# Attention and an MLP-mixer in one kernel: the first pass in another order

## The chip, the cores and the metric

The kernel runs on one core of a Trainium2 chip. The metric is the device time of one execution in microseconds, lower is better. Engines are named as in the profile: PE is TensorE's matmul, PEld its weight load, DVE is VectorE, ACT is ScalarE, POOL is GpSimd and SP is SyncE, which here only issues DMAs.

## The reference

```python
# q, k, v: (8, 8, 576, 64) float32, g_norm: (64,); the mixer's four weights are float64
kv  = einsum('bhsd,bhse->bhde', k, v)
out = einsum('bhsd,bhde->bhse', q, kv)
rms = sqrt(mean(out * out, axis=-1) + 1e-6)
x   = (out / rms * g_norm) as (8, 576, 512)        # heads side by side
h   = maximum(x.T @ w_tok1, 0) @ w_tok2            # over the 576 tokens; 256 wide
u   = x + h.T
y   = u + maximum(u @ w_ch1, 0) @ w_ch2            # over the 512 channels; 1536 wide
```

## The kernel before, in words

**First stage.** Batches are taken two at a time: four pairs. Of each batch, 512 rows lie in four tiles of 128, and the remaining 64 rows of both batches of a pair share a fifth. `attention(pair)` has nine steps. `kv(side, half)` multiplies half of the heads' k and v (`ps_kv`), copies the two diagonal blocks into `kvp` (one copy on DVE, one on ACT), and asks for the next k and v (`load(n + 2)`; two buffers each). `attend(c)` is 8 matmuls into `ps_o` for two row tiles; `attend_rem` does the shared tile. Each ends in `norm`: a square on ACT, a sum, a root with one step of correction and a product on DVE, the product with `g_norm` on POOL. That gives one tile of `X`.

`token_mixing(pair)` has 11 steps: `tok1(t)`, for half of the 256 columns, sums over all row tiles of both batches and over the shared tile into `ps_h`, then applies the maximum on ACT (`h1`); `tok2(i)` makes row tile i of u in `ps_u`, DVE adds X, and a DMA stores u in `u_dram`.

**The weights** arrive as float64. `decode` rounds a block to float32: a scaled copy on ACT, a clip on POOL (L134), four operations on DVE (L136, L138, L140, L142) and a last add on POOL (L144). The raw blocks come by DMAs on ACT's queue into two buffers (`raw`). Both channel products use a 2 x 2 scheme with seven products, for which `mix_ch1` and `mix_ch2` form four sums each of the rounded weights, on POOL (L185, 1536 columns each).

**Order of the first stage.** `weave(body, fill)` writes body's steps and spreads the others between them. The first attention is woven with the token weights, then the mixing of pair p with the attention of pair p + 1, and over the three of these the blocks of w_ch1 (eight of 768 columns), `mix_ch1`, the blocks of w_ch2 (twelve of 512), `mix_ch2`. The last mixing is woven with the first transposes of u. A scheduler may then move instructions on an engine; the order of each engine is fixed when the program is built, and each engine works through its own in that order.

**Channel stage.** Nine groups of 512 rows of u: `channel1` for three parts of the hidden width (`ps_v`), then `channel2` (`ps_w`), with the transposes of the next group between.

Of the kernel before, what the change touches and what calls it, by code (L numbers as in the profile page):

```python
# [9 lines left out]
F32 = mybir.dt.float32  # L10
# [7 lines left out]
def kernel(  # L18
# [55 lines left out]
    dram = ctx.enter_context(tc.tile_pool(name="dram", bufs=1, space=bass.MemoryType.DRAM))  # L74
    right = ExitStack()
# [26 lines left out]
    def w_psum(shape, name):  # L102
        return ps_w.tile(shape, F32, name=name, tag="w")

# [3 lines left out]
    def load(n):  # L108
# [40 lines left out]
    def fetch(n):  # L149
        return stage.tile([P, n, 2], U32, name="raw", tag="raw")  # L150

    def get_tok1(j, n):
        raw = fetch(n * DTOK)
        w = words(moe_w_tok1)
        if j < J:
            nc.scalar.dma_start(raw.rearrange("p (j n) w -> p j n w", j=n),
                                w[ds(j * P, n * P)].rearrange("(j p) n w -> p j n w", p=P))
        else:
            nc.scalar.dma_start(raw[:HF], w[LO:])
            nc.scalar.dma_start(raw[HF:], w[LO:])  # L160
        decode(w_tok1[:, j:j + n].rearrange("p j n -> p (j n)"), raw)

    def get_tok2(t):
        raw = fetch(S)
        nc.scalar.dma_start(raw, words(moe_w_tok2)[ts(t, P)])
        decode(w_tok2[:, t], raw)
# [6 lines left out]
    def get_ch1(i, c):  # L173
        raw = fetch(FH)
        nc.scalar.dma_start(raw, words(moe_w_ch1)[ts(c, P), ts(i, FH)])
        decode(w_ch1[:, A1[i, c // 2], c % 2], raw)

    def get_ch2(f):
        raw = fetch(DM)
        nc.scalar.dma_start(raw, words(moe_w_ch2)[ts(f, P)])  # L180
        a, b = B2[f // NS, 0], B2[f // NS, 1]
        decode(w_ch2[:, a:b + 1:b - a, f % NS], raw.rearrange("p (h n) w -> p h n w", h=2))

    def combine(o, a, b, op):
        nc.gpsimd.tensor_tensor(out=o, in0=a, in1=b, op=op)  # L185

    def mix_ch1():
        w = [w_ch1[:, i] for i in range(7)]
# [5 lines left out]
    def mix_ch2():  # L194

        w = [w_ch2[:, i] for i in range(7)]
# [12 lines left out]
    def attention(pair):  # L209
        def kv(side, half):  # L210
            n = 4 * pair + 2 * side + half
            kk, vv = k_in[n % 2], v_in[n % 2]
            ps = w_psum([P, 2, P], "ps_kv")
            for i in range(2):
                for j in range(JJ):
                    nc.tensor.matmul(ps[:, i], lhsT=kk[:, j, ts(i, P)], rhs=vv[:, j, ts(i, P)],  # L216
                                     start=(j == 0), stop=(j == JJ - 1))
            dst = kvp[side][:, 2 * half:2 * half + 2]
            nc.vector.tensor_copy(dst[:HF, :, :D], ps[:HF, :, :D])
            nc.scalar.copy(dst[HF:, :, D:], ps[HF:, :, D:])  # L220
# [25 lines left out]
        def attend(c):  # L246
            side = c // 2
            ps = ps_o.tile([P, 2, DM], F32, name="ps_o", tag="o")
            for t in range(2):
                for hp in range(HP):  # L250
                    nc.tensor.matmul(ps[:, t, ts(hp, P)],  # L251
                                     lhsT=qT[2 * pair + side][:, hp, ts(2 * (c % 2) + t, P)],
                                     rhs=kvp[side][:, hp], start=True, stop=True)
            norm(ps, c, 2)

        def attend_rem():
            ps = ps_o.tile([P, 1, DM], F32, name="ps_o", tag="o")
            for hp in range(HP):
                for side in range(2):
                    nc.tensor.matmul(ps[ds(side * HF, HF), 0, ts(hp, P)],  # L260
                                     lhsT=qT[2 * pair + side][:, hp, LO:],
                                     rhs=kvp[side][:, hp], start=True, stop=True)
            norm(ps, 4, 1)

        return [do(kv, 0, 0), do(kv, 0, 1), do(attend, 0), do(kv, 1, 0), do(attend, 1),
                do(kv, 1, 1), do(attend_rem), do(attend, 2), do(attend, 3)]


    def token_mixing(pair):
        h1 = {}  # L270

        def tok1(t):
            ps = []
            for side in range(2):
                if t == 0:
                    h1[side] = hp_.tile([P, NTOK, DM], F32, name="h1")
                ps.append(w_psum([P, DM], "ps_h"))
                for j in range(J):
                    nc.tensor.matmul(ps[side], lhsT=w_tok1[:, j, ts(t, P)],  # L279
                                     rhs=x_of(pair, side * J + j), start=(j == 0), stop=False)  # L280
            for side in range(2):
                r = ds(side * HF, HF)
                nc.tensor.matmul(ps[side], lhsT=w_tok1[r, J, ts(t, P)], rhs=x_of(pair, 8)[r],
                                 start=False, stop=True)
            for side in range(2):
                nc.scalar.activation(h1[side][:, t], ps[side], AF.Relu)  # L286

        def tok2(i):
            ps = w_psum([P, DM], "ps_u")
            if i < 8:  # L290
                for t in range(NTOK):
                    nc.tensor.matmul(ps, lhsT=w_tok2[:, t, ts(i % J, P)], rhs=h1[i // J][:, t],  # L292
                                     start=(t == 0), stop=(t == NTOK - 1))
            else:
                for t in range(NTOK):
                    for side in range(2):
                        nc.tensor.matmul(ps[ds(side * HF, HF)], lhsT=w_tok2[:, t, LO:],
# [3 lines left out]
            nc.vector.tensor_tensor(out=x, in0=ps, in1=x, op=ALU.add)  # L301
# [7 lines left out]
        return [do(tok1, t) for t in range(NTOK)] + [do(tok2, i) for i in range(9)]  # L309
# [9 lines left out]
    def turn_u(g, i, psum):  # L319
        if i == 0:  # L320
            uT[g] = late["u"].tile([P, NC, J * P], F32, name="uT")
        ps = psum()
        for c in range(NC):
            nc.tensor.transpose(ps[:, c], xg[g][:, i, ts(c, P)], ident)  # L324
        nc.scalar.copy(uT[g][:, :, ts(i, P)], ps)  # L325
# [216 lines left out]
```

## Time and profile before

| | us |
|---|---|
| runs | 976.95, 981.16, 983.23 (median 981.16) |
| profiled execution | 976.97 |
| its span | 975.2 |
| PE busy | 896.6 (92%) |
| DVE busy | 383.1 (39%) |
| POOL busy | 246.2 (25%) |
| ACT busy | 148.5 (15%) |
| first matmul of the channel stage | 302.2 |

The span is the time from the first to the last instruction. Shares are of the whole span, of which the channel stage is the larger part; a share within the first stage has to be read from a window of it. A busy PE may run at a lower granted clock, which is listed apart. HBM traffic of the whole span is 52.85 MB read and 18.87 MB written.

### The profile page before, as it was taken

The page shows a single profiled execution, that of the slowest core. Times are in us where ns is not written, and L with a number is a line of the kernel's source. Part 1 is how long each engine was busy: PE and PEld are TensorE (multiplying, and loading weights), DVE is VectorE, ACT ScalarE, POOL GpSimd, SP SyncE. Part 2 cuts the span into 40 slices and gives each one's busy share as a digit, 9 for nine tenths or more (in the row PEclk, how much of TensorE's full clock was granted, in tenths as well). Part 3 has the DMA queues.
Part 4 walks back from the last instruction along what each step waited for, and adds up shares of the span by engine and source line. Part 5 has one row for each costly group of instructions (what it writes and reads, how often), then busy time and mean ns, then how long its engine had stood idle before and what let it go on. Part 6 is the DMA issues. An engine that isn't in the chain of part 4 may idle for free.

```text
span 975.2 us, 10020 instructions
## 1 busy us (share of the span) xinstructions
PE 896.6 (92%) x4128; PEld 723.8 (74%) x4128; DVE 383.1 (39%) x573; ACT 148.5 (15%) x252; POOL 246.2 (25%) x169
## 2 busy tenths in 40 slices
PE   3749669769999999999999999999999999999997
PEld 2525434535636888888888888888888888888886
DVE  2876887791724303413413412312313312312421
ACT  1321211211211101201201201200210210210210
POOL 2464666470210220220220220220220220220220
PEclk9879879889999999999999999999999999999999
DMA  9955654553332002002002002002002001001001
GB/s 263 317 170 175 223 196 152 189 199 95 118 133 76 1 1 87 1 1 87 1 0 87 1 1 87 1 1 85 3 1 76 10 1 44 1 1 44 1 1 43
DMA packets 42413, 72.37 MB, mean 74 GB/s; under 512 B 2560, under 2 KB 20992, under 8 KB 42368
## 3 DMA queue, kind: packets, MB, share of 16 engines
q1 hardware_dynamic: 38352, 56.63, 17.6%
q10 hardware_dynamic: 4016, 15.11, 4.7%
q8 instruction: 32, 0.52, 0.2%
q14 instruction: 13, 0.11, 0.0%
HBM read 52.85 MB, written 18.87 MB: 74 GB/s over the span
## 4 chain that ended last, share of the span: by engine, by line
PE 78%; DVE 11%; DMA 4%; POOL 4%; issue 1%; ACT 1%; SPq 0%; ACTq 0%; DVEq 0%; POOLq 0%
PE ps_v L365 33%; PE ps_w L404 33%; PE ps_u L292 3%; DMA raw<-in_moe_w_ch_dram 3%; PE ps_h L279 3%; PE ps_kv L216 2%; DVE part L142 2%; PE ps_ut L324 2%; POOL w_ch L185 1%; POOL x L244 1%; DVE x L243 1%; PE ps_o L251 1%; DVE w_ch L138 1%; DVE part L140 1%; DVE ms L230 1%
## 5 line engine op out<-in xcount | busy, mean ns | idle before, releaser
L365 PE MATMUL ps_v<-uT,w_ch 128*128 128x256 f32 x864 | 201.3, 379 | 0.0
L404 PE MATMUL ps_w<-w_ch,vs 128*128 128x256 f32 x864 | 192.1, 379 | 0.0
L365 PEld LDWEIGHTS ps_v<-uT,w_ch 128*128 128x128 f32 x864 | 164.1, 190 | 23.1 <-issue 0.8
L404 PEld LDWEIGHTS ps_w<-w_ch,vs 128*128 128x128 f32 x864 | 162.3, 190 | 21.1
L393 POOL TENSOR_TENSOR vs<-vs,v 128x512 f32<-128x512 f32 x27 | 47.6, 1764 | 428.3 <-DVE vs L389 410.4
L365 PE MATMUL ps_v<-t,w_ch 128*128 128x256 f32 x648 | 153.1, 379 | 0.0
L404 PE MATMUL ps_w<-w_ch,v 128*128 128x256 f32 x648 | 144.1, 379 | 0.0
L365 PEld LDWEIGHTS ps_v<-t,w_ch 128*128 128x128 f32 x648 | 123.1, 190 | 16.7
L404 PEld LDWEIGHTS ps_w<-w_ch,v 128*128 128x128 f32 x648 | 122.5, 190 | 16.3
L279 PE MATMUL ps_h<-x,w_tok 128*128 128x512 f32 x128 | 65.5, 654 | 16.4 <-POOL x L244 16.4
L369 DVE TENSOR_TENSOR v<-ps_v,u 128x512 f32<-128x512 f32 x54 | 37.3, 692 | 102.1 <-PE ps_v L365 102.1
L251 PE MATMUL ps_o<-kvp,qT 128*128 128x128 f32 x256 | 40.2, 319 | 30.4 <-DVE x L243 17.7
L409 POOL TENSOR_TENSOR xg<-xg,u 128x512 f32<-128x512 f32 x27 | 33.8, 1266 | 135.3 <-DVE u L408 135.3
L251 PEld LDWEIGHTS ps_o<-kvp,qT 128*128 128x128 f32 x256 | 37.7, 228 | 40.5 <-issue 23.0
L279 PEld LDWEIGHTS ps_h<-x,w_tok 128*128 128x128 f32 x128 | 25.0, 208 | 52.9 <-issue 29.0
L292 PE MATMUL ps_u<-h,w_tok 128*128 128x512 f32 x128 | 61.8, 614 | 1.4 <-ACT h L286 1.4
L408 DVE TENSOR_TENSOR xg<-ps_w,xg 128x512 f32<-128x512 f32 x27 | 18.7, 692 | 104.9 <-PE ps_w L404 104.9
L244 POOL TENSOR_TENSOR x<-x,g_sb 128x1024 f32<-128x1024 f32 (+1 forms) x20 | 44.2, 2210 | 61.4 <-DVE x L243 58.6
L216 PEld LDWEIGHTS ps_kv<-v_in,k_in 128*128 128x128 f32 x320 | 41.0, 206 | 20.8 <-issue 19.5
L216 PE MATMUL ps_kv<-v_in,k_in 128*128 128x128 f32 x320 | 42.1, 291 | 13.9 <-DMA v_in<-in_v_dram 13.9
L325 ACT COPY uT<-ps_ut 128x512 f32<-128x512 f32 x36 | 21.1, 586 | 213.2 <-PE ps_ut L324 213.2
L408 DVE TENSOR_TENSOR u<-ps_w,u 128x512 f32<-128x512 f32 x18 | 12.4, 692 | 87.2 <-PE ps_w L404 87.2
(62 smaller groups left out, 680.6 us busy)
## 6 DMA issues: line engine op xcount, KB each, us to landing
qT<-in_q_dram SPq DMA_DIRECT2D x8, 1152.0 KB, 5.7
xg<-u_dram SPq DMA_DIRECT2D x9, 1024.0 KB, 5.6
k_in<-in_k_dram SPq DMA_DIRECT2D x16, 512.0 KB, 5.4
v_in<-in_v_dram SPq DMA_DIRECT2D x16, 512.0 KB, 6.7
u_dram<-x SPq DMA_DIRECT2D x16, 512.0 KB, 3.0
out_dram<-xg SPq DMA_DIRECT2D x16, 512.0 KB, 2.8
raw<-in_moe_w_ch_dram ACTq DMA_DIRECT2D x8, 768.0 KB, 4.4
raw<-in_moe_w_ch_dram ACTq DMA_DIRECT2D x12, 512.0 KB, 4.4
```

The source lines that it names most:

```text
L216: nc.tensor.matmul(ps[:, i], lhsT=kk[:, j, ts(i, P)], rhs=vv[:, j, ts(i, P)], start=(j == 0), stop=(j == JJ - 1))
L244: nc.gpsimd.tensor_mul(x3, x3, g_sb.to_broadcast([P, n * H, D]))
L251: nc.tensor.matmul(ps[:, t, ts(hp, P)], lhsT=qT[2 * pair + side][:, hp, ts(2 * (c % 2) + t, P)], rhs=kvp[side][:, hp], start=True, stop=True)
L279: nc.tensor.matmul(ps[side], lhsT=w_tok1[:, j, ts(t, P)], rhs=x_of(pair, side * J + j), start=(j == 0), stop=False)
L292: nc.tensor.matmul(ps, lhsT=w_tok2[:, t, ts(i % J, P)], rhs=h1[i // J][:, t], start=(t == 0), stop=(t == NTOK - 1))
L325: nc.scalar.copy(uT[g][:, :, ts(i, P)], ps)
L365: nc.tensor.matmul(ps[:, w], lhsT=w_ch1[:, n - 1, c, ts(W * d + w, P)], rhs=uc[g][n - 1][:, c], start=(start and w == 0 and c == 0), stop= ...
L369: add = lambda o, ps, x: nc.vector.tensor_tensor(out=o, in0=ps, in1=x, op=ALU.add)
L393: nc.gpsimd.tensor_tensor(out=s2, in0=s1, in1=a11, op=ALU.subtract)
L404: nc.tensor.matmul(ps[:, p], lhsT=V[g, s // 2][n - 1][:, s % 2, ts(p, P)], rhs=w_ch2[:, n - 1, s], start=(start and p == 0 and s == 0), st ...
L408: add = lambda o, ps, y: nc.vector.tensor_tensor(out=o, in0=ps, in1=y, op=ALU.add)
L409: padd = lambda o, a, b: nc.gpsimd.tensor_tensor(out=o, in0=a, in1=b, op=ALU.add)
```

## The change

1. `attention` and `token_mixing` give their steps by name, and the order is written out. For a mixing beside the next attention it is `kv00 h00 kv01 h01 a0 h10 h11 hr kv10 a1 kv11 u0 u1 r u2 u3 a2 u4 u5 u6 a3 u7 u8`. Here `h` with side and t is a quarter of the first token matmul (one batch now, not both), `hr` the shared tile's part of all four quarters, `u` a step of `tok2`, `a` an `attend`, `r` the shared tile's.
2. PSUM: `ps_o` has one buffer of two banks, not two; the remainder (`ps_r`) and `ps_kv` have one each, `ps_h` and `ps_u` share four.
3. All loads of weights go to SP's queue, the token weights ahead of the first attention's rounding (two of them into the buffers of `h1`); `raw` has three buffers. q of a batch is asked for with the second half of its k and v, not with the first.
4. w_ch1 comes in sixteen blocks of 384 columns. w_ch2's blocks are written after the third mixing: half of them in the last mixing, half in group 0's `channel1`. The sums move to DVE, in pieces: eight of 768 columns for w_ch1, twelve of 512 for w_ch2.

```diff
+    stage = pool("stage", 2, "right")
...
-    stage = pool("stage", 2, "left", left)
...
-    ps_o = pool("ps_o", 2, "left", psums, space=bass.MemoryType.PSUM)
-    ps_w = pool("ps_w", 4, "left", psums, space=bass.MemoryType.PSUM)
+    ps = {n: pool(f"ps_{n}", b, "left", psums, space=bass.MemoryType.PSUM)
+          for n, b in (("o", 1), ("r", 1), ("kv", 1), ("h", 4))}
...
-        if half == 0:
+        if half == 1:
             dst = qT[b] = qtp.tile([P, HP, S], F32, name="qT")
...
+    def block(n, loads, dst, turn=lambda raw: raw, home=None):
+        raw = []
+        def fetch():
+            if home is None:
+                raw.append(stage.tile([P, n, 2], U32, name="raw", tag="raw", bufs=3))
+            else:
+                raw.append(home.tile([P, n, 2], U32, name="raw", tag="h1"))
+            for o, i in loads(raw[0]):
+                nc.sync.dma_start(o, i)
+        return fetch, lambda: decode(dst, turn(raw[0]))
...
+    def get_ch1(i, c, h):
+        return block(FQ, lambda raw: [(raw, words(moe_w_ch1)[ts(c, P), ts(2 * i + h, FQ)])],
+                     w_ch1[:, A1[i, c // 2], c % 2, ts(h, FQ)])
...
     def combine(o, a, b, op):
-        nc.gpsimd.tensor_tensor(out=o, in0=a, in1=b, op=op)
+        nc.vector.tensor_tensor(out=o, in0=a, in1=b, op=op)
...
-        return [do(kv, 0, 0), do(kv, 0, 1), do(attend, 0), do(kv, 1, 0), do(attend, 1),
-                do(kv, 1, 1), do(attend_rem), do(attend, 2), do(attend, 3)]
+        steps = {f"kv{s}{h}": do(kv, s, h) for s in range(2) for h in range(2)}
+        steps |= {f"a{c}": do(attend, c) for c in range(4)} | {"r": attend_rem}
+        return steps
...
+    first = run("kv00 kv01 a0 kv10 a1 kv11 r a2 a3", attention(0))
+    both = ("kv00 h00 kv01 h01 a0 h10 h11 hr kv10 a1 kv11 u0 u1 r u2 u3 a2 u4 u5 u6 a3 u7 u8")
+    last = "h00 h01 h10 h11 hr u0 u1 u2 u3 u4 u5 u6 u7 u8"
...
+    for fetch, _ in tok:
+        fetch()
+    weave(first, [round_ for _, round_ in tok])
     steps = []
     for pair in range(B // 2 - 1):
-        weave([do(steps.append, f) for f in token_mixing(pair)],
-              [do(steps.append, f) for f in attention(pair + 1)])
-    weave(steps, weights)
+        steps += run(both, attention(pair + 1), token_mixing(pair))
+    weave(steps, staggered(ch1) + [do(mix_ch1, c) for c in range(2)])
...
+    weights = [w for i in range(3) for w in staggered(ch2[4 * i:4 * i + 4]) + mixes[i]]
+    cut = len(weights) // 2
...
+    weave(steps[:5], weights[:cut // 3])
...
+        weave([do(channel1, g, d) for d in range(NS // 2)], weights[cut:] if g == 0 else [])
```

What stands in each engine's order, at three places. PE where pair 0's mixing ends and pair 1's begins, before (`ps_o` is an attention, `ps_h` the first token matmul, `ps_u` the second, `ps_kv` the key-value product):

```order
L292 MATMUL ps_u<-h_370,w_tok_87 128x512 x2
L251 MATMUL ps_o<-kvp_95,qT 128x128 x8
L297 MATMUL ps_u<-h_364,w_tok_87 64x512
L297 MATMUL ps_u<-h_370,w_tok_87 64x512
L297 MATMUL ps_u<-h_364,w_tok_87 64x512
L297 MATMUL ps_u<-h_370,w_tok_87 64x512
L251 MATMUL ps_o<-kvp_95,qT 128x128 x8
L279 MATMUL ps_h<-x,w_tok_86 128x512 x4
L283 MATMUL ps_h<-x,w_tok_86 128x512
L279 MATMUL ps_h<-x,w_tok_86 128x512 x5
```

The same place a pair later in the changed kernel, where pair 1's mixing ends with a3 and pair 2's begins:

```order
L259 MATMUL ps_o<-kvp_101,qT 128x128 x8
L307 MATMUL ps_u<-h_777,w_tok_93 64x512
L307 MATMUL ps_u<-h_780,w_tok_93 64x512
L307 MATMUL ps_u<-h_777,w_tok_93 64x512
L307 MATMUL ps_u<-h_780,w_tok_93 64x512
L224 MATMUL ps_kv<-v_in_98,k_in_96 128x128 x10
L284 MATMUL ps_h<-x,w_tok_92 128x512 x4
L224 MATMUL ps_kv<-v_in_99,k_in_97 128x128 x10
L284 MATMUL ps_h<-x,w_tok_92 128x512 x4
L259 MATMUL ps_o<-kvp_100,qT 128x128 x8
L284 MATMUL ps_h<-x,w_tok_92 128x512 x8
```

Before, the first token matmuls of both batches follow the last attention at once. Now two key-value products, the first batch's quarters and the next a0 stand between a3 and the second batch's quarters, which read what a3 gives.

The sums of weights: POOL before, around the four of w_ch1 (L244 is the product with `g_norm`, L134 and L144 belong to `decode`):

```order
L144 TENSOR_TENSOR w_ch_88<-w_ch_88,part 128x768 x2
L134 TENSOR_SCALAR w_ch_88<-w_ch_88 128x768
L134 TENSOR_SCALAR w_ch_89<-w_ch_89 128x2x256
L244 TENSOR_TENSOR x<-x,g_sb 128x1024
L144 TENSOR_TENSOR w_ch_88<-w_ch_88,part 128x768
L185 TENSOR_TENSOR w_ch_88<-w_ch_88 128x1536 x4
L244 TENSOR_TENSOR x<-x,g_sb 128x1024
```

DVE in the changed kernel, around the second four of w_ch1, at the end of pair 1's mixing (L193 is the sum, L238 to L251 the normalisation of a3, L227 the copy into `kvp`, L311 the add of X):

```order
L238 TENSOR_REDUCE ms<-x 128x16
L311 TENSOR_TENSOR x<-ps_u,x 128x512
L239 TENSOR_SCALAR ms<-ms 128x16
L193 TENSOR_TENSOR w_ch_94<-w_ch_94 128x768
L245 RECIPROCAL inv<-root 128x16
L193 TENSOR_TENSOR w_ch_94<-w_ch_94 128x768
L246 SCALAR_TENSOR_TENSOR ms<-ms,inv 128x16
L227 COPY kvp_100<-ps_kv 64x2x64
L248 SCALAR_TENSOR_TENSOR root<-root,ms 128x16
L193 TENSOR_TENSOR w_ch_94<-w_ch_94 128x768
L250 RECIPROCAL inv<-root 128x16
L193 TENSOR_TENSOR w_ch_94<-w_ch_94 128x768
```

The sums no longer stand ahead of a product on POOL; they stand between the operations of a normalisation on DVE. Further on in DVE's order, the last rounding and the last sums of w_ch2 stand ahead of the last mixing's adds, and none in the channel stage.

SP's queue, which held loads of k, v and q and stores of u before (there at the start of the third mixing):

```order
L114 DMA k_in_90<-in_k_dram 128x4x256
L115 DMA k_in_90<-in_k_dram 64x256
L114 DMA v_in_92<-in_v_dram 128x4x256
L115 DMA v_in_92<-in_v_dram 64x256
L114 DMA k_in_91<-in_k_dram 128x4x256
L115 DMA k_in_91<-in_k_dram 64x256
L114 DMA v_in_93<-in_v_dram 128x4x256
L115 DMA v_in_93<-in_v_dram 64x256
L305 DMA u_dram_98<-x 128x2x512
```

And in the changed kernel, from the end of pair 0's mixing on:

```order
L313 DMA u_dram_110<-x 128x512
L111 DMA k_in_96<-in_k_dram 128x4x256
L112 DMA k_in_96<-in_k_dram 64x256
L111 DMA v_in_98<-in_v_dram 128x4x256
L112 DMA v_in_98<-in_v_dram 64x256
L156 DMA raw<-in_moe_w_ch_dram 128x768
L111 DMA k_in_97<-in_k_dram 128x4x256
L112 DMA k_in_97<-in_k_dram 64x256
L111 DMA v_in_99<-in_v_dram 128x4x256
L112 DMA v_in_99<-in_v_dram 64x256
L156 DMA raw<-in_moe_w_ch_dram 128x768 x6
L111 DMA k_in_96<-in_k_dram 128x4x256
```

The raw blocks of the weights, six on end at one place, now stand among the loads of k and v.

More of the change, by code (lines that the diff above doesn't have):

```diff
@@ L265, in attention @@
-        return [do(kv, 0, 0), do(kv, 0, 1), do(attend, 0), do(kv, 1, 0), do(attend, 1),
-                do(kv, 1, 1), do(attend_rem), do(attend, 2), do(attend, 3)]
+            norm(o, 4, 1)
+        steps = {f"kv{s}{h}": do(kv, s, h) for s in range(2) for h in range(2)}
+        steps |= {f"a{c}": do(attend, c) for c in range(4)} | {"r": attend_rem}
+        return steps
     def token_mixing(pair):
-        h1 = {}
-        def tok1(t):
-            ps = []
-            for side in range(2):
[L275 to L286, printed above, removed]
+        h1, acc = {}, {}
@@ L300, in tok2 @@
             x = x_of(pair, i)
[L301 removed]
+            nc.vector.tensor_tensor(out=x, in0=acc_u, in1=x, op=ALU.add)
             if i == 8:
```

114 lines of the change are left out of this document (62 added, 52 removed).

## The prediction

> **What bounds the kernel now.** I read the page's slices first, then a table of stretches, then the chain of waits inside the first stretches.
>
> ```profile
> span 975.2 us, 10020 instructions
> ...
> PE   3749669769999999999999999999999999999997
> ...
> GB/s 263 317 170 175 223 196 152 189 199 95 118 133 76 1 1 87 1 1 87 1 0 87 1 1 87 1 1 85 3 1 76 10 1 44 1 1 44 1 1 43
> ```
>
> A slice is 24.4 us. TensorE (PE) is full from slice 10 on and has holes before it; nearly all bytes move in the first twelve slices. The stretches below are cut where the token matmuls of pairs 0, 1, 2, 3 and the channel stage begin (columns: PE, weight load, DVE, ACT, POOL busy with counts, granted clock, DMA share, GB/s):
>
> ```profile
> 0.00:46.00 46.00, 22.73 (x140) 20.10 (x141) 23.78 (x43) 10.56 (x17) 16.23 (x23) 0.93 0.96 291
> 46.00:137.70 91.70, 62.66 (x263) 37.74 (x263) 71.46 (x99) 18.34 (x32) 54.09 (x31) 0.82 0.57 187
> 137.70:212.50 74.80, 57.17 (x242) 34.32 (x242) 61.04 (x88) 14.68 (x27) 44.78 (x29) 0.89 0.58 190
> 212.50:265.20 52.70, 51.61 (x242) 30.26 (x242) 23.28 (x48) 9.09 (x18) 10.68 (x5) 0.99 0.32 108
> 265.20:302.20 37.00, 35.40 (x97) 14.44 (x96) 13.79 (x22) 5.86 (x10) 4.69 (x2) 1.00 0.38 135
> 302.20:975.20 673.00, 667.03 (x3154) 586.97 (x3152) 189.76 (x277) 89.96 (x149) 115.70 (x81) 1.00 0.07 25
> ```
>
> The channel stage is 673.0 us with PE busy 667.0: nothing in this change makes it shorter. All that can move is the first 302.2 us. There the same work (one attention beside one token mixing, 242 matmul records) takes 74.8 us while weights are rounded and 52.7 us once they are done; the first time, with 263 records, 91.7 us. In the slow stretches DVE is busy 71.5 and 61.0 us, and the clock is 0.82 and 0.89.
>
> What PE needs, from the chain where it ran without waits:
>
> ```profile
> 236.17 2.23 PE ps_kv L216 x20
> ...
> 240.12 1.78 PE ps_o L251 x16
> ...
> 256.74 1.02 PE ps_o L260 x16
> ...
> 277.48 6.21 PE ps_h L279 x14
> 283.68 1.06 PE ps_h L283 x4
> ...
> 290.53 0.44 PE ps_ut L324 x4
> 290.97 3.44 PE ps_u L292 x8
> ...
> 300.43 1.87 PE ps_u L297 x8
> ```
>
> One pair is 4 x 2.23 (key-value) + 4 x 1.78 + 1.02 (attention) + 32 x 0.444 + 8 x 0.265 (first token matmul) + 32 x 0.43 + 1.87 (second) = 49.0 us; the last mixing alone, with four transposes, is 33.7. Four pairs and the transposes need about 198 us of the 302.
>
> Why the rest is lost:
>
> ```profile
> 112.08 14.18 POOL L185 TENSOR_TENSOR w_ch<-w_ch 128x1536 f32<-128x1536 f32 x4
> ...
> 116.39 3.11 DVE L238 SCALAR_TENSOR_TENSOR ms<-ms,inv 128x16 f32<-128x16 f32 x1
> 119.43 0.27 DVE L219 COPY kvp<-ps_kv 64x128 f32<-64x128 f32 x1
> 119.63 3.27 DVE L240 SCALAR_TENSOR_TENSOR root<-root,ms 128x16 f32<-128x16 f32 x1
> ...
> 120.05 1.11 PE L260 MATMUL ps_o<-kvp,qT 128*64 128x128 f32 x6 [8.54 <-ACT kvp L220]
> ...
> 134.14 3.76 PE L251 MATMUL ps_o<-kvp,qT 128*128 128x128 f32 x16 [5.62 <-DVE x L243]
> ```
>
> POOL sums weights, four times 3.5 us on end. Two 16-column DVE operations take 3.1 and 3.3 us in that time, the copy of kvp stands behind one of them in DVE's order, and PE waits 8.5 us for it. Then PE waits 5.6 us for a normalisation, and its next 16 records take 3.76 us, not 1.78.
>
> **The change, part by part.** Times are against the profiled execution: span 975.2, its own time 976.97, which is 4.2 under the median of the three runs.
>
> *Attention spread out.* By the order, key-value blocks, 16 records of attention and tok1 now alternate, and a3 (the pair's last attention) stands two key-value blocks, two tok1 groups and a0 ahead of the first matmul that reads its X: 2 x 2.23 + 2 x 3.55 + 1.78 = 13.3 us. The chain behind a3 is one normalisation. Its DVE rows, from a stretch without rounding:
>
> ```profile
> L301 DVE TENSOR_TENSOR x<-ps_u,x 128x512 f32<-128x512 f32 x17 | 11.7, 686 | 26.6 <-PE ps_u L292 26.6
> L230 DVE TENSOR_REDUCE ms<-x 128x16 f32<-128x1024 f32 x4 | 4.9, 1217 | 5.2 <-ACT x L228 5.2
> L243 DVE TENSOR_TENSOR x<-ps_o,inv 128x1024 f32<-128x1024 f32 x4 | 4.8, 1212 | 0.1
> ...
> L330 DVE TENSOR_TENSOR t<-uT,t 128x512 f32<-128x512 f32 x2 | 1.4, 688 | 0.0
> ...
> L237 DVE RECIPROCAL inv<-root 128x16 f32<-128x16 f32 x4 | 1.0, 252 | 1.1 <-ACT root L235 1.1
> L219 DVE COPY kvp<-ps_kv 64x128 f32<-64x128 f32 x4 | 1.0, 251 | 16.8 <-PE ps_kv L216 16.8
> L240 DVE SCALAR_TENSOR_TENSOR root<-root,ms 128x16 f32<-128x16 f32 x4 | 0.7, 174 | 0.1
> ```
>
> 1.22 + 1.21 + 2 x 0.25 + 3 x 0.17 = 3.44 us on DVE, with some 1 us of ACT ahead and 2.35 of POOL behind. It fits in 13.3. The new single buffer ps_o is the added wait: a2 must be normalised before a3 starts. Four second-token matmuls lie between them (4 x 1.72 = 6.9 us), against about 5 us of ACT and DVE. That cover is thin: a rounding of 2.2 us ahead of it on DVE is enough to make PE wait, and u8 and the next kv00 are queued behind a3.
>
> *Weight rounding and sums.* DVE does four operations per block; those of 512 columns, early, with POOL quiet:
>
> ```profile
> 10.16 0.43 DVE L136 TENSOR_SCALAR w_tok<-w_tok 128x512 uint32<-128x512 uint32 x1 [8.22 <-POOL w_tok L134]
> 10.63 0.69 DVE L138 SCALAR_TENSOR_TENSOR w_tok<-raw,w_tok 128x512 uint32<-128x512 uint32 x1
> ...
> 16.41 0.41 DVE L140 TENSOR_SCALAR part<-w_tok 128x512 uint32<-128x512 uint32 x1
> ...
> 17.08 0.68 DVE L142 SCALAR_TENSOR_TENSOR part<-raw,part 128x512 f32<-128x512 uint32 x1
> ```
>
> That is 2.2 us. A block of 384 columns isn't in the trace: between 3/4 of it (1.66) and all of it (2.2); I take 1.75, near the proportion. A sum on DVE has the form of L330: 0.69 for 512 columns, and for 768 between 0.69 and 1.03; I take 1.0. So 28 us leave POOL and 8 x 1.0 + 12 x 0.69 = 16 us come to DVE.
>
> DVE then has per pair 4 x 3.44 + half of that and a little for the remainder (2.1) + 9 x 0.69 + 4 x 0.25 = 23.1 us. By the order, pair 0's mixing is joined by 7 blocks of w_ch1 (12.3), pair 1's by 9 of them, one of w_ch2 and 8 sums (26.0), pair 2's by 10 of w_ch2 and 9 sums (28.2): 35.4, 49.1 and 51.3 us.
>
> To this comes what POOL costs DVE. Up to 212.5 DVE was busy 156.3 us (first three stretches), while quiet durations give 118 (ten large and three small normalisations 40.7, 18 adds 12.4, copies 3, eight blocks of 768 at 3.1, twelve of 512, 10.7 for the token weights). The 38 us left lie beside POOL's two-input work:
>
> ```profile
> L244 POOL TENSOR_TENSOR x<-x,g_sb 128x1024 f32<-128x1024 f32 (+1 forms) x20 | 44.2, 2210 | 61.4 <-DVE x L243 58.6
> ...
> L144 POOL TENSOR_TENSOR w_ch<-w_ch,part 128x512 f32<-128x512 f32 (+1 forms) x20 | 33.3, 1666 | 29.6 <-DVE part L142 29.6
> ```
>
> By then POOL had done 26 us of L244, 33 of L144 (6 more for the token weights) and 28 of L185, some 94: 0.40 us of DVE per us of POOL. Without L185 a pair has 10.7 us of the g products plus 1.0 per small and 1.27 per large block: 18, 21 and 23 us, so 7, 8 and 9 on DVE.
>
> The Trainium skill, SBUF — State Buffer, section "SBUF: two separate sides", says that VectorE and GpSimd take a shared port pair as an exclusive lock for a whole instruction, also for a VectorE operation with two SBUF inputs. The 3.1 and 3.3 us above agree; the rule speaks against the sums on VectorE, since each would shut out POOL in turn. If each POOL operation stopped DVE for its whole length, the three pairs would get 18, 21 and 23 us and the pairs would take 53, 70 and 74 us and the first stage 271; by the measured 0.40 it is what follows.
>
> DVE per pair: 42, 57 and 60 us, against PE's 49. DVE keeps one order, so the pairs take 49, 57 and 60.
>
> *Loads.* The start must bring k, v, q and token weights of pair 0, 9.6 MB, and 13.2 MB until q of the next pair: by the page's first two slices (263 and 317 GB/s, 14.1 MB in 48.8 us) at 34 and 46 us. Pair 1's a0 can start then, and it stands 11.6 us of PE work into the new cycle, so the cycle starts between 35 us and, with the normalisation of a3 ahead of a0, some 42. I take 40.
>
> *Second channel weight later.* By the order, every rounding and sum of w_ch2 stands on DVE ahead of the last mixing's adds, so it costs the channel stage nothing. Were six blocks and eight sums left to group 0, 6 x 2.2 + 8 x 0.69 = 19 us beside that group's 21 us of DVE (189.8 / 9) in 74.8 us, they would cost up to 10.
>
> Sum: 40 + 49 + 57 + 60 + 33.7 = 240; with 673.0 the span is 913, the execution 915. As a median, between that and 4 above: **917**.
>
> **Rivals.** (1) DVE doesn't bind: its listed durations overlap by some hundredths, and rounding fills its idle time. Then PE sets all pairs: 40 + 3 x 49 + 33.7 = 221, time 896. For it: 52.7 us at 212.5 with all its work; against: 23.3 us of DVE there.
> (2) DVE is no denser than in 137.7 to 212.5, 61.0 of 74.8: it waits for square roots, raw blocks and POOL's clip in its order. Pairs of 52, 70 and 74 give 269, time 944. Three raw buffers in place of two and earlier loads speak against it.
> (3) Slower: one queue carries all. Every raw load waits on SP for a rounding three blocks back, and k, v, q and the stores of u queue behind it, where the weights had ACT's queue. Until the last k, v some 46 MB must pass (28.3 of k, v, q, 2.5 and 8 of weights, 7 of u), and 57 us of PE work follow (23 of the last pair, 33.7). At 279 GB/s, below, nothing is lost; at 187, the second stretch's rate, the stage lasts 246 + 57 = 303, no gain; below about 180 it is slower: at 170, 328 us and a time of 1003.
>
> ```profile
> 236.00:246.00 10.00, 10.00 (x66) 7.96 (x65) 4.23 (x10) 1.50 (x3) 0.00 (x0) 1.00 0.85 279
> ```
>
> There SP's queue ran alone. The Trainium skill, DMA: Bandwidth & Descriptors, section "Issuing engines are not separate DMA queues", says that queues of several engines share the same 16 DMA engines and only save issue time: by it the one queue costs nothing. This row agrees.
> (4) The new order isn't what runs, since a scheduler decides: excluded by the order, as far as the program goes.
>
> **How the numbers follow.** Forecast (905 to 932) 0.50, rival 1 0.20, rival 2 0.22, rival 3 0.08, half of it within 1% and half slower. The range takes rivals 1 and 2: 893 to 950. A measurement of this kernel tells about 1% from no change. Faster 0.92, same 0.04, slower 0.04.
>
> **What would show it.** The channel stage again 673 us; its first matmul at about 240; the last two pairs longer than the first, with DVE over 90% busy in them, the wait at a3 on L251 and no DVE operation of 16 columns over 2.5 us. Wrong, if PE waits on k_in, v_in or qT, if the pairs are all 49, or if channel2 of group 0 waits for w_ch.

## The result, and the profile after

The changed kernel takes 937.12 us (936.45 to 937.48), the kernel before 981.54 us (976.95 to 983.23) beside it on the same chip: a ratio of 0.9554 (0.9521 to 0.9587), 44 us faster. Times here are medians of four executions with the lowest and the highest in brackets; behind a ratio to the kernel before stands its 95% interval. The forecast was 64 us faster, 917, in a range of 893 to 950. Direction and bound were right; the first stage was forecast at 240 us and lasts 261.9.

The page of the changed kernel, its span, the slices of PE and DVE, and what the queues carried:

```profile
span 934.6 us, 10129 instructions
...
PE   4698979968999999999999999999999999999997
...
DVE  2858789899343133124123223213314303412411
...
q1 hardware_dynamic: 43376, 71.71, 23.0%
```

A slice is now 23.4 us. PE still has holes in the first ten slices, and DVE reads 7 to 9 in eight of them. One queue carries all 71.7 MB.

Stretches, cut where the shared tile's part of the first token product (`hr`) of pairs 0, 1, 2 and 3 ends and where the channel stage begins (columns: PE, weight load, DVE, ACT, POOL busy with counts, granted clock, DMA share, GB/s):

```profile
0.00:67.90 67.90, 46.58 (x257) 35.19 (x257) 37.16 (x70) 14.72 (x27) 24.45 (x26) 0.92 0.83 264
67.90:123.20 55.30, 51.09 (x243) 30.84 (x241) 45.57 (x84) 14.35 (x30) 28.03 (x25) 0.97 0.70 229
123.20:183.70 60.50, 53.07 (x242) 32.98 (x240) 55.07 (x99) 14.59 (x29) 28.55 (x25) 0.92 0.71 233
183.70:244.30 60.60, 48.16 (x187) 27.70 (x185) 52.72 (x85) 11.67 (x22) 30.09 (x22) 0.89 0.45 152
244.30:261.90 17.60, 17.60 (x58) 8.07 (x56) 7.54 (x12) 3.69 (x7) 0.00 (x0) 1.00 0.28 102
261.90:934.60 672.70, 667.01 (x3154) 587.99 (x3152) 190.87 (x279) 89.91 (x149) 115.85 (x81) 1.00 0.07 25
```

The forecast in these cuts. A mixing's part up to `hr` is 16.3 us of PE work. With the two key-value products and a0 that stand beside it (2 x 2.23 + 1.78 = 6.2 us) it is 22.6 us of a cycle of 49.0. So 40 + 22.6 = 62.6 was forecast for the first stretch, then 49, 57 and 60, the last less the 6.2 us of attention that no longer stand there (53.8), and 17.6. Measured are 67.9, 55.3, 60.5, 60.6 and 17.6: over by 5.3, 6.3, 3.5 and 6.8, together 22. In what follows the middle three are called pair 1, pair 2 and pair 3.

In the three pairs DVE is busy 45.57 + 55.07 + 52.72 = 153.4 us, against 159 in the forecast, but 87% of 176.4 us. What DVE waited for in them (us in total, times, longest):

```profile
DVE w_ch L133 <- POOL w_ch L131: 13.1, 5, 5.1
DVE w_ch L193 <- POOL w_ch L141: 3.9, 3, 1.4
DVE inv L245 <- ACT root L243: 2.9, 5, 1.6
DVE ms L238 <- ACT x L236: 1.3, 1, 1.3
DVE part L137 <- POOL w_ch L141: 0.9, 1, 0.9
DVE kvp L227 <- PE ps_kv L224: 0.5, 1, 0.5
```

And the longer waits of PE in its timeline (start, us, line, count, in brackets the idle time before and what ended it):

```profile
28.36 2.50 PE L259 MATMUL ps_o<-kvp,qT 128*128 128x128 f32 x10 [8.85 <-DVE x L251]
...
94.76 2.61 PE L259 MATMUL ps_o<-kvp,qT 128*128 128x128 f32 x16 [3.34 <-DVE x L251]
...
132.62 4.57 PE L224 MATMUL ps_kv<-v_in,k_in 128*128 128x128 f32 x20 [5.17 <-ACT kvp L228]
...
156.19 2.60 PE L259 MATMUL ps_o<-kvp,qT 128*128 128x128 f32 x16 [2.27 <-DVE x L251]
...
197.25 4.63 PE L224 MATMUL ps_kv<-v_in,k_in 128*128 128x128 f32 x20 [9.23 <-ACT kvp L228]
...
222.63 3.50 PE L259 MATMUL ps_o<-kvp,qT 128*128 128x128 f32 x16 [2.97 <-DVE x L251]
```

Three waits are the expected ones, a3 behind the normalisation of a2. The first, 8.85 us, is a1 of pair 0 behind the normalisation of a0. The largest two of the pairs were not named: a key-value product waits until `ps_kv` is copied into `kvp`, and the copy (L227 on DVE, then L228 on ACT) stands behind roundings, and in pair 3 behind three sums too. What follows a wait is slow: 20 records of the key-value product took 2.23 us before where PE ran through, and 4.57 and 4.63 here.

### The profile page after: what moved, and what is told of

Its sections match the earlier page's. It is cut to its first block, busy times and chain, and to the rows that moved or that the text cites. A ratio compares the mean times of both kernels' runs of the same rounds, so it can differ in the third digit from the quotient of the medians.

```text
span 934.6 us, 10129 instructions
## 1 busy us (share of the span) xinstructions
PE 883.5 (95%) x4128; PEld 722.8 (77%) x4128; DVE 388.9 (42%) x625; ACT 148.9 (16%) x260; POOL 227.0 (24%) x177
## 4 chain that ended last, share of the span: by engine, by line
PE 80%; DVE 13%; DMA 3%; issue 2%; POOL 2%; ACT 1%; SPq 0%; DVEq 0%; ACTq 0%
PE ps_v L376 35%; PE ps_w L415 35%; PE ps_h L284 3%; PE ps_u L302 2%; PE ps_kv L224 2%; DVE part L137 2%; PE ps_ut L335 2%; DVE x L251 2%; DVE ms L238 1%; DVE x L311 1%; DVE part L139 1%; DMA raw<-in_moe_w_tok_dram 1%; DVE w_ch L135 1%; PE ps_o L259 1%; DVE w_ch L193 1%
## 5 line engine op out<-in xcount | busy, mean ns | idle before, releaser
L224 PE MATMUL ps_kv<-v_in,k_in 128*128 128x128 f32 x320 | 47.6, 315 | 27.4 <-ACT kvp L228 18.0
L224 PEld LDWEIGHTS ps_kv<-v_in,k_in 128*128 128x128 f32 x320 | 45.3, 227 | 34.5 <-ACT kvp L228 19.7
L302 PE MATMUL ps_u<-h,w_tok 128*128 128x512 f32 x128 | 58.7, 604 | 0.0
L284 PE MATMUL ps_h<-x,w_tok 128*128 128x512 f32 x128 | 57.7, 596 | 0.6 <-POOL x L252 0.5
L252 POOL TENSOR_TENSOR x<-x,g_sb 128x1024 f32<-128x1024 f32 (+1 forms) x20 | 45.3, 2266 | 51.8 <-DVE x L251 38.0
L259 PEld LDWEIGHTS ps_o<-kvp,qT 128*128 128x128 f32 x256 | 33.9, 210 | 24.1 <-issue 13.9
L259 PE MATMUL ps_o<-kvp,qT 128*128 128x128 f32 x256 | 35.9, 298 | 17.4 <-DVE x L251 17.4
L284 PEld LDWEIGHTS ps_h<-x,w_tok 128*128 128x128 f32 x128 | 23.3, 190 | 26.5 <-issue 23.4
```

The lines of the kernel that those rows point to most:

```text
L224: nc.tensor.matmul(acc[:, i], lhsT=kk[:, j, ts(i, P)], rhs=vv[:, j, ts(i, P)], start=(j == 0), stop=(j == JJ - 1))
L252: nc.gpsimd.tensor_mul(x3, x3, g_sb.to_broadcast([P, n * H, D]))
L259: nc.tensor.matmul(o[:, t, ts(hp, P)], lhsT=qT[2 * pair + side][:, hp, ts(2 * (c % 2) + t, P)], rhs=kvp[side][:, hp], start=True, stop=True)
L284: nc.tensor.matmul(acc[side, t], lhsT=w_tok1[:, j, ts(t, P)], rhs=x_of(pair, side * J + j), start=(j == 0), stop=False)
L302: nc.tensor.matmul(acc_u, lhsT=w_tok2[:, t, ts(i % J, P)], rhs=h1[i // J][:, t], start=(t == 0), stop=(t == NTOK - 1))
```

## The experiments

The theory was that DVE's work in the pairs sets the first stage. Its rivals: single places in the order (a copy behind a rounding, one PSUM buffer), the one queue, or the order of steps as such. All kernels below are the changed kernel with an edit, but for one. The times of the kernel before beside them were 978.35 to 981.53. The line numbers of kernels with added lines are 7 to 9 higher.

**Copies into `kvp` both on ACT.**

```diff
-            nc.vector.tensor_copy(dst[:HF, :, :D], acc[:HF, :, :D])
+            nc.scalar.copy(dst[:HF, :, :D], acc[:HF, :, :D])
```

> The changed kernel with both copies into kvp on ACT; before, one of the two stood in DVE's order. Theory A (place in the order): PE's waits ahead of kv11, 5.2 and 9.2 us in pairs 2 and 3 with 2 us each of half clock behind them, come from that copy standing behind rounding on DVE; without it the time falls to 915 to 924. Theory B (amount of DVE work): pairs last as long as DVE's work, and only 1 us of copies per pair leaves DVE; the waits move to a3 and r, and the time stays within 931 to 937.

938.63 us (938.33 to 939.24), ratio 0.9575 (0.9560 to 0.9589): no gain, somewhat above theory B's bracket. Pairs 1 and 2 end 4.2 us earlier (179.5, not 183.7), pair 3 gives it back:

```profile
179.48:247.17 67.69, 51.29 (x185) 28.58 (x185) 55.07 (x86) 11.88 (x24) 31.73 (x22) 0.87 0.39 136
```

PE now waits in other places of pair 3:

```profile
204.57 3.75 PE L259 MATMUL ps_o<-kvp,qT 128*128 128x128 f32 x16 [7.25 <-DVE x L251]
...
237.12 8.12 PE L284 MATMUL ps_h<-x,w_tok 128*128 128x512 f32 x12 [4.09 <-POOL x L252]
```

**Two buffers for `ps_kv`**, one less for `ps_h` and `ps_u`.

```diff
-          for n, b in (("o", 1), ("r", 1), ("kv", 1), ("h", 4))}
+          for n, b in (("o", 1), ("r", 1), ("kv", 2), ("h", 3))}
```

> The changed kernel with two buffers for ps_kv and three, not four, for ps_h and ps_u. Theory A: kv11 no longer waits for kv10's copy, but r, 3.4 us of PE work later, still needs both copies: about half of the 14 us comes back, 925 to 932. Theory B: 933 to 938. A third outcome: three banks for ps_u make tok2 wait for DVE's adds, 940 or more.

937.52 us (934.74 to 937.72), ratio 0.9554 (0.9532 to 0.9576), inside theory B's bracket. The waits moved to the remainder's attention (4.0 and 3.8 us) and to `h` (2.4). In both experiments one row stayed. It is the last product of the last normalisation in DVE's timeline, in the changed kernel and then with the copies on ACT:

```profile
233.27 1.22 DVE L251 TENSOR_TENSOR x<-ps_o,inv 128x1024 f32<-128x1024 f32 x1
```

```profile
233.06 1.22 DVE L251 TENSOR_TENSOR x<-ps_o,inv 128x1024 f32<-128x1024 f32 x1
```

With two `ps_kv` it is 233.20. DVE gets to the end of its work of attention at the same time whichever wait of PE is taken away.

**Channel weights not rounded.** Four operations of `decode` on DVE and the last add on POOL left out for `w_ch1` and `w_ch2`.

```diff
+        if not full:
+            return
         nc.vector.tensor_scalar(out=bits, in0=bits, scalar1=3, scalar2=None,
...
-                     w_ch1[:, A1[i, c // 2], c % 2, ts(h, FQ)])
+                     w_ch1[:, A1[i, c // 2], c % 2, ts(h, FQ)], full=False)
```

> The changed kernel without the four DVE operations and the last POOL add of rounding for w_ch1 and w_ch2 (left out; the ACT copy and POOL's clip stay, the sums stay). If DVE's work and what POOL costs it bound the pairs, PE sets them: 49 each after a start of 46, channel stage at 227 to 235, time 900 to 909. If loads or SP's order bound them, the time stays above 925.

908.74 us (908.20 to 910.35), ratio 0.9272 (0.9256 to 0.9287). Pairs 1, 2 and 3:

```profile
68.20:117.50 49.30, 49.20 (x243) 29.95 (x241) 24.68 (x49) 15.25 (x31) 17.71 (x19) 1.00 0.91 292
117.50:173.90 56.40, 50.90 (x242) 31.46 (x242) 35.94 (x64) 17.72 (x32) 22.25 (x18) 0.97 0.88 285
173.90:218.30 44.40, 43.18 (x185) 23.74 (x185) 21.25 (x43) 7.98 (x16) 11.09 (x8) 1.00 0.36 124
```

In pairs 1 and 3 PE is busy 49.20 of 49.30 and 43.18 of 44.40 us at full clock: this is PE's floor of a pair, near the forecast's 49.0 and 42.8 (49.0 less 6.2). Pair 2 is 7 us above it, although DVE is busy only 35.9 of 56.4 us there. It holds most of the sums, DVE waits 10.9 us for POOL's clip ahead of them, and a copy into `kvp` that stands behind eight sums holds PE:

```profile
127.12 3.90 PE L226 MATMUL ps_kv<-v_in,k_in 128*128 128x128 f32 x20 [5.40 <-ACT kvp L230]
```

So most of the loss goes with the rounding, but place in DVE's order still costs PE time when its amount is small. In pair 1 the loads ran at 292 GB/s, and after the start PE waited for none.

**Sums on POOL again**, in the small pieces.

```diff
-        nc.vector.tensor_tensor(out=o, in0=a, in1=b, op=op)
+        nc.gpsimd.tensor_tensor(out=o, in0=a, in1=b, op=op)
```

> The changed kernel with the sums of weights back on POOL, in the same small pieces (1.75 us for 768 columns, 1.2 for 512). By the amount of DVE work: 16 us leave DVE's order and 28 x 0.4 = 11 come back as time behind POOL: 930 to 937. By the order of the port (each POOL operation stops one DVE operation for its length, and the sums stand ahead of the g products): slower, 940 to 950.

956.05 us (955.67 to 957.24), ratio 0.9754 (0.9738 to 0.9769): 19 us lost, above both brackets. The sums in the groups of the first stage, on DVE in the changed kernel, and here on POOL:

```profile
L193 DVE TENSOR_TENSOR w_ch<-w_ch 128x512 f32<-128x512 f32 (+1 forms) x20 | 18.6, 948 | 3.9 <-POOL w_ch L141 3.9
```

```profile
L193 POOL TENSOR_TENSOR w_ch<-w_ch 128x512 f32<-128x512 f32 (+1 forms) x20 | 31.1, 1571 | 0.8
```

18.6 us of sums left DVE, yet it was busy 193.65 us before the channel stage, against 198.06: only 4.4 less. So 14.2 us of other DVE work came in their place, 0.46 us for each of POOL's 31.1. The amount of DVE's work doesn't explain the 19 us, then. The waits grew: in the pairs DVE waited 19.6 us for POOL's clip (13.1 in the changed kernel), and PE waited longer for the copies of `kvp` (22.0 us, not 17.3) and at the end for the product with g, which stood behind three sums on POOL:

```profile
254.00 7.92 PE L284 MATMUL ps_h<-x,w_tok 128*128 128x512 f32 x12 [4.28 <-POOL x L252]
```

That is the second theory's way of being slower, and more than it put on it.

**Second half of `w_ch2` held until the last mixing is done**: seven blocks and eight sums queued on DVE behind the last mixing's last add.

```diff
-            nc.vector.tensor_tensor(out=x, in0=acc_u, in1=x, op=ALU.add)
+            ins = nc.vector.tensor_tensor(out=x, in0=acc_u, in1=x, op=ALU.add)
+            if (pair, i) == (3, 8):
+                gate.append(ins.ins)
...
+    weights[cut:] = [held(w) for w in weights[cut:]]
```

> The second half of w_ch2 (seven blocks of 512 columns and eight sums, by quiet rows 7 x 2.2 + 8 x 0.69 = 21 us of VectorE) is issued on VectorE only behind the last add of the last mixing, so it stands in the channel stage of group 0. Theory A (the amount of DVE work in the pairs sets the first stage): pair 3, 60.6 us now, falls to near its 43 us of PE work, say 45 to 49, and the channel stage starts at 248 to 252; if the channel stage hides the work, as DVE is busy only 21 of 74.8 us per group there, the time is 921 to 927. Theory B (the work can't be hidden there: adds of channel1 queue behind a block, or channel2 of group 0 waits for w_ch): the channel stage is up to 10 us longer than 672.7 and the time is 929 to 937.

939.43 us (937.59 to 939.86), ratio 0.9574 (0.9548 to 0.9600), above both brackets. Pair 3, the rest of the last mixing, and the channel stage:

```profile
185.65:238.78 53.13, 45.64 (x185) 25.99 (x185) 28.09 (x50) 9.02 (x18) 16.98 (x11) 0.90 0.38 134
238.78:256.33 17.55, 17.55 (x56) 8.00 (x57) 6.64 (x10) 3.64 (x7) 0.00 (x0) 1.00 0.28 102
256.33:937.40 681.07, 670.63 (x3154) 588.72 (x3152) 218.63 (x315) 92.01 (x153) 128.45 (x92) 0.99 0.08 28
```

Pair 3 fell from 60.6 to 53.1, with DVE busy only 28.1 us of it (theory A said 45 to 49), and the channel stage pays 8.4 us, 681.07 against 672.70: both theories were half right. The channel stage hides only part of the work, though DVE has much idle time there; one add came late enough to hold PE for 4.4 us:

```profile
281.94 3.78 PE L385 MATMUL ps_v<-t,w_ch 128*128 128x256 f32 x8 [4.37 <-DVE u L389]
```

**The same work held only until the last attention's normalisation**, so that it lies beside the last mixing. The edit is the same, with the gate at the product L251 of a3 in pair 3.

> The same seven blocks and eight sums are issued on VectorE only behind the last normalisation of attention (a3 of pair 3), so they lie beside the last mixing, where DVE is now idle for some 20 of 28 us. Theory A (amount of DVE work in the pairs): pair 3 loses up to 21 us of DVE and its waits on kvp and ps_o; the last mixing gets about 29 us of DVE work in some 28 us of PE work, so it is 0 to 6 us longer; time 922 to 930. Theory B (what counts is the chain raw load, ACT, POOL, DVE, POOL of a block, not the amount): the adds of the last mixing queue behind blocks that wait for POOL and raw, all is given back, time 933 to 940.

934.89 us (934.32 to 935.41), ratio 0.9531 (0.9506 to 0.9555), short of the first bracket. Pair 3 and the rest of the last mixing:

```profile
183.95:237.55 53.60, 45.36 (x186) 25.92 (x185) 38.77 (x64) 10.39 (x20) 21.73 (x15) 0.90 0.44 153
237.55:260.07 22.52, 19.94 (x58) 8.49 (x57) 20.37 (x32) 4.88 (x9) 8.50 (x8) 0.92 0.28 98
```

7.0 us won, 4.9 paid. With DVE busy 38.8 of 53.6 us, amount no longer explains pair 3; what is left is a wait that stands ahead of the held work:

```profile
196.29 4.63 PE L231 MATMUL ps_kv<-v_in,k_in 128*128 128x128 f32 x20 [8.13 <-ACT kvp L235]
```

**Steps in the order of before.**

```diff
-    both = ("kv00 h00 kv01 h01 a0 h10 h11 hr kv10 a1 kv11 u0 u1 r u2 u3 a2 u4 u5 u6 a3 u7 u8")
+    both = ("h00 h10 h01 h11 hr kv00 u0 kv01 u1 a0 u2 kv10 u3 u4 a1 u5 kv11 u6 r u7 a2 u8 a3")
```

> Everything as changed, but the steps of a pair in the order of before (the four tok1 groups first, attention behind them, a3 last), with the changed buffers, loads and sums. If the amount of DVE work alone sets the pairs, the order is worth nothing: 934 to 942. If spreading attention is a gain of its own, PE waits at each h10 and hr for the normalisation of a3 that stands just ahead (some 5 us each, four times) and kv, u and a steps wait as in the kernel before: 950 to 965.

936.59 us (935.94 to 938.96), ratio 0.9554 (0.9522 to 0.9586): with the rest of the change in place, the order is worth nothing. PE's waits between 20 and 275 us, as sums:

```profile
PE ps_o L259 <- DVE x L251: 14.0, 6, 8.8
PE ps_kv L224 <- ACT kvp L228: 6.3, 2, 3.6
PE ps_h L284 <- POOL x L252: 6.3, 6, 1.8
PE ps_r L268 <- ACT kvp L228: 3.8, 3, 1.9
PE ps_h L291 <- POOL x L252: 2.4, 3, 1.0
```

The waits for X that the new order avoids are there, but small (8.7 us, 0.5 in the changed kernel), and the copies of `kvp` cost less (10.1 us, 17.3 in the changed kernel).

**Raw blocks on ACT's queue.**

```diff
-                nc.sync.dma_start(o, i)
+                nc.scalar.dma_start(o, i)
```

> The raw blocks are loaded from ACT's queue again, k, v, q and the stores of u stay on SP. If the one queue costs nothing, as the 9.4 us at the start are PE's only wait on a load: 934 to 940. If k, v, q or raw blocks are late because they share a queue, it is faster, 920 to 930. If ACT, which must issue a load only once a raw buffer is free, holds its copies and square roots behind that wait, it is slower, 945 to 960.

949.79 us (948.25 to 950.96), ratio 0.9682 (0.9656 to 0.9709): 12.7 us slower. The edit also let the engines' orders fall out otherwise: 13 of the sixteen blocks of w_ch1 are now rounded before pair 0's `hr` ends, where the changed kernel has none. So `hr` ends at 90.9 us, not 67.9, and pair 3, with little DVE work left, is down to PE's floor:

```profile
214.70:257.70 43.00, 42.90 (x186) 23.67 (x185) 18.32 (x39) 7.02 (x15) 8.34 (x4) 1.00 0.37 128
```

What was measured is in good part another order of DVE's work. No gain from a second queue shows, but what the one queue costs by itself stays open.

**Token weights held behind the first normalisations.**

```diff
-    weave(first, [round_ for _, round_ in tok])
+    weave(first, rounds[:1] + [held(f, 0, 0) for f in rounds[1:3]] + [held(f, 0, 1) for f in rounds[3:]])
```

> VectorE's roundings of the token weights after the first are issued behind the normalisation of a0 (two of them) and of a1 (the last two) of pair 0. Nothing is left out. In the changed kernel a1 waits 8.85 us for the normalisation of a0, whose small operations stand between roundings (20.75 to 28.31 us). If that wait is why the start is 5.8 us above the forecast, a1 begins at about 24 to 25 in place of 28.4, and the channel stage starts 3 to 6 us earlier: 931 to 934. If the roundings are then late for the first token matmul, or the pairs behind take the time back as VectorE has the same work in them, the time stays at 936 to 939.

935.87 us (934.12 to 937.77), ratio 0.9546 (0.9517 to 0.9576). The wait at the start, now for the whole of the second attention:

```profile
26.82 3.78 PE L267 MATMUL ps_o<-kvp,qT 128*128 128x128 f32 x16 [7.39 <-DVE x L258]
```

It begins 1.5 us sooner, pair 0's `hr` ends 0.9 sooner (67.0), and the channel stage begins at 263.2. The reason given for the start fell: with the other roundings out of the way, the chain from the square of a0's normalisation to its product still takes 7.3 us (19.47 to 26.77).

**Without the product with g** on POOL.

```diff
-            nc.gpsimd.tensor_mul(x3, x3, g_sb.to_broadcast([P, n * H, D]))
```

> Leaves out the product with g on POOL behind each normalisation (45.3 us of POOL's two-input work in the first stage). If POOL's two-input work costs VectorE 0.40 us per us of it, as the prediction put it, VectorE is busy some 18 us less before the channel stage (about 180 in place of 198), 13 of them in the three pairs, and the time is 922 to 928. If VectorE and POOL hardly hold each other up, VectorE's busy time stays within 5 us and only the wait for x behind POOL goes: 933 to 937.

918.49 us (917.44 to 920.62), ratio 0.9365 (0.9333 to 0.9397), below the lower bracket. The three pairs:

```profile
66.30:118.16 51.86, 49.44 (x241) 30.00 (x241) 39.77 (x88) 14.38 (x30) 17.24 (x20) 1.00 0.76 249
118.16:174.18 56.02, 51.78 (x242) 32.42 (x241) 48.37 (x96) 14.96 (x29) 16.84 (x21) 0.94 0.77 251
174.18:228.54 54.36, 46.09 (x185) 25.99 (x185) 46.43 (x84) 11.62 (x22) 18.98 (x17) 0.94 0.50 169
```

DVE does the same operations in 134.6 us, not 153.4. Over the whole first stage it is 176.7 against 198.1: 21.4 us for 45.3 us of POOL, 0.47. The three pairs take 162.2 us in place of 176.4, although DVE's waits for POOL's clip did not shrink (15.1 us, 13.1 in the changed kernel). One group shows it bare, first in the changed kernel, then here:

```profile
L239 DVE TENSOR_SCALAR ms<-ms 128x8 f32<-128x8 f32 x4 | 4.4, 1103 | 0.1
```

```profile
L239 DVE TENSOR_SCALAR ms<-ms 128x8 f32<-128x8 f32 x4 | 0.7, 163 | 0.1
```

**The kernel before with its sums on DVE**, nothing else changed (eight operations of 1536 columns).

```diff
-        nc.gpsimd.tensor_tensor(out=o, in0=a, in1=b, op=op)
+        nc.vector.tensor_tensor(out=o, in0=a, in1=b, op=op)
```

> The kernel before with one part of the change alone: the weight sums on VectorE (eight operations of 1536 columns). If the 14.2 us of four POOL sums on end, which stretched 16-column operations to 3.1 and 3.3 us, are a loss of their own, and 19 us were lost where the changed kernel had its sums on POOL again, the time is 958 to 968. If the sums cost VectorE as much as they give back, 976 to 982.

970.34 us (967.73 to 974.37), ratio 0.9901 (0.9864 to 0.9938): 10.5 us, between the two brackets. The sums are worth 10 us alone and 19 as the last part of the change. DVE does them in 14.7 us and is still busy less before the channel stage (189.75 us against 193.35): 18.3 us of its other work went with POOL's 27.8 us, 0.66.

**Copies on ACT together with the held half**, the first and the sixth experiment in one.

> The copies into kvp on ACT (as in the first experiment, where the wait only moved) together with the second half of w_ch2 held on VectorE behind the last normalisation of attention. Nothing is left out. Theory A (place in VectorE's order matters only once its amount leaves slack): pair 3, 53.6 us with the hold alone, still waited 8.13 us for the copy; without that wait it falls to 44 to 47, the last mixing stays at 22.5, and the time is 925 to 930. Theory B (the wait moves on again, to a normalisation or to h): pair 3 stays above 51 and the time is 933 to 939.

924.75 us (922.71 to 925.02), ratio 0.9444 (0.9423 to 0.9465): faster than both kernels, with nothing left out, and at the edge of theory A's bracket. Pair 3, the rest of the last mixing, and the channel stage:

```profile
178.95:227.85 48.90, 45.32 (x185) 24.53 (x185) 39.37 (x63) 10.70 (x22) 22.37 (x15) 0.97 0.50 168
227.85:250.36 22.51, 20.00 (x56) 8.48 (x56) 20.36 (x32) 4.86 (x9) 8.50 (x8) 0.92 0.28 98
250.36:923.10 672.74, 667.00 (x3154) 586.97 (x3152) 191.83 (x280) 90.11 (x149) 116.02 (x81) 1.00 0.07 26
```

The copies alone gained nothing and the hold 2 us; together they gain 12 (by the ratios 11), five of them ahead of pair 3, as with the copies alone, and not given back. Pair 3 is not quite down to theory A's 44 to 47. Its wait for the copy is 1.79 us at 184.95, and the row of the last normalisation, seen above at 233, stands here at

```profile
214.09 1.22 DVE L258 TENSOR_TENSOR x<-ps_o,inv 128x1024 f32<-128x1024 f32 x1
```

That row in the kernels that do all the work of the changed one, and last in the two with work left out, beside the end of the first stage:

| kernel | last product of a3, pair 3 | channel stage begins |
|---|---|---|
| changed | 233.3 | 261.9 |
| copies on ACT | 233.1 | 264.7 |
| two `ps_kv` | 233.2 | 263.0 |
| order of before | 235.3 | 262.2 |
| token weights held | 233.7 | 263.2 |
| held to the channel stage | 225.0 | 256.3 |
| held to the last mixing | 223.8 | 260.1 |
| held, and copies on ACT | 214.1 | 250.4 |
| raw blocks on ACT's queue | 244.0 | 275.3 |
| sums on POOL again | 246.9 | 281.4 |
| without the product with g | 217.7 | 246.1 |
| channel weights not rounded | 204.5 | 235.8 |

With a copy, a buffer, the order of steps or the start changed (the first five lines), the row stays within 2 us of the changed kernel's. Where work left pair 3 it moves by 8 to 10, with DVE busy 24.6 and 14.0 us less there, and once DVE has slack a better place is worth 10 more. Two other places of the same work moved it back by 11 and 14 us: a place can cost much even where it gains nothing.

## Why the prediction was right, and where its size was off

**Right, by its own steps.** The channel stage is 672.7 us. PE's only wait for a load is the 9.4 us at the start. PE's floor of a pair is 49 us, as pair 1 of the kernel without rounding shows. DVE's order bounds the pairs: without the product with g DVE is busy 18.8 us less in the three pairs, they take 14.2 us less, and the kernel 18.6. But the amount of work is not the whole bound: pair 3 took 54.4 us with 46.4 of DVE (without g), 69.5 with 45.7 (sums on POOL) and 53.1 with 28.1 (held to the channel stage). The normalisation of a3 fits in its 13.3 us, since PE waits for X at pair boundaries for 0.3 us at most, but that was worth nothing in the end. a3's cover was thin: 3.3, 2.3 and 3.0 us. No 16-column operation takes longer than 1.3 us, where 3.1 and 3.3 had stood, and no rounding is in the channel stage.

**The terms of DVE.** Sums of 768 columns took 1.12 us and of 512 0.84, not 1.0 and 0.69: 18.6 us in place of 16. Blocks took longer too, with POOL's cost in them. Together the pairs hold 153.4 us of DVE, forecast 159: the amount was right to 4%. The 0.40 us of DVE per us of POOL is 0.47 (product with g taken away), 0.46 (sums put back) and 0.66 (sums taken away in the kernel before). POOL's 45.3 us of products cost DVE 21.4, not 45.3, as the prediction's 271 us for the first stage would have needed. The Trainium skill, SBUF — State Buffer, "SBUF: two separate sides", gives the shared port to one instruction for its whole length. Over a stage that rule doesn't price POOL's time one for one, by these runs.

**The step that failed**: "DVE keeps one order, so the pairs take 49, 57 and 60". It made a pair's time the larger of two sums of work, as if DVE worked without a gap. DVE was busy 82%, 91% and 87%, so the sign of over 90% in the last two pairs came in one; the six kinds of waits shown sum to 22.6 us, 13.1 of them a rounding that waits for POOL's clip and 3.9 a sum that waits for POOL's last add. Rival 2 named these waits ("square roots, raw blocks and POOL's clip in its order") and put 82% on every pair, which is too much; the truth lies between. Against it the forecast set three raw buffers and earlier loads. Yet ACT, which hands each block to POOL's clip, waited 34.0 us for raw blocks between 20 and 275 us, 7.4 us of them just ahead of the longest wait for the clip (5.1 us). So PE's waiting for no load doesn't show that late raw blocks cost nothing.

From PE's side the pairs add up so: 140.8 us of work at full clock, 24.1 of waits (15.3 for copies into `kvp`, 8.6 for a3, 0.2 for X), and 11.5 by which its records are longer (51.1 + 53.1 + 48.2 us busy). Together they are the 176.4 us measured, 17 over the forecast. The forecast left PE 19 us of waiting for DVE (159.8 less 140.8) and put the slower records at nothing, though it had seen some (3.76 us for 1.78). Pair 1 shows it best: DVE has only 45.6 us of work there, and 4.2 us of waits and 2.1 of slower records still bring PE from 49 to 55.3. What DVE's gaps are worth is read from the trace, as no run took them away alone; not all 22.6 us count, since 6.5 of them lie behind the last normalisation, where PE waits 0.25 us.

**The other term**: the start, 5.3 us late (the expectation above has 5.8). The forecast took it from the bytes to be loaded. From PE's side its 67.9 us are 9.4 until the first load is there, 39.6 of work (17.1 for pair 0's attention, 22.6 as above), 11.8 of other waits, 8.8 of them a1 behind the normalisation of a0, and 7.0 by which records are longer. Moving the token roundings away from that normalisation gave 0.9. In the changed kernel and in eight of the experiments the start ends between 66 and 69 us, whether rounding, sums, g, copies or the hold were changed; with two `ps_kv` it is 70.7 and with raw blocks on ACT's queue 90.9. What would shorten it is open: no run took that wait away. 42, the upper end of the forecast's bounds, would have been nearer than 40.

**Parts of the 44 us.** The order gave nothing, and the sums 10 to 19. The queue's part couldn't be told from that of DVE's order (12.7 us for both). PSUM buffers, three raw buffers, smaller blocks, earlier loads and the later place of w_ch2 were not tried one by one, so where the rest comes from is not shown.

**Work left to the channel stage**: costed at up to 10 us for six blocks and eight sums, it was 8.4 for seven and eight.

## What to carry to other kernels

When an in-order engine is the bound, price its waits as well as its work, and what the engine behind it loses after each wait: here DVE was busy 87%, and the wait of PE for a copy, taken away alone in two ways, came back elsewhere. Look for one row late in that engine's order that does not move from kernel to kernel; when it stays, take work away, and only then mend places. Idle time of an engine in a later stage isn't free for deferred work if that stage's adds queue behind it.

## What the runs showed of the hardware

- POOL's two-input work costs DVE about half its time or more: 0.47, 0.46 and 0.66 us per us, by three edits. The 8-column operation of DVE shown above takes 0.16 us on average without the product with g on POOL, and 1.10 with it. Taking 45 us of work off POOL, which was busy 42% of the first stage, made the kernel 18.6 us faster.
- A wait costs PE more than its length: after 5.2 and 9.2 us of idling, the next 20 records took 4.6 us in place of 2.2, at a granted clock of 0.52 and 0.51, and after 3.0 us (222.63) the next 16 took 3.50 in place of 1.78, at 0.56. After 3.3 and 2.3 us (94.76 and 156.19) they took 2.6, at 0.74. The Trainium skill, TensorE: Matmul & The Clock Gate, "Part 1: The HAM clock gate (the "warmup" mystery)", says that the clock halves after an idle window of about 3.4 us. The rows agree, but a wait somewhat shorter was enough here. Before the channel stage PE is busy 216.5 us for the forecast's 198 of work; the 18.5 us more are 2% of the span.
